# Delta-rule attention and cosine-routed experts in one kernel: units of two sequences on a written schedule, paired 64x64 products, an 8-row base of the triangular inverse

## Chip, cores and metric

The kernel runs on one core of a Trainium2 chip. The metric is device time in microseconds; the program runs once per measurement, and the figure for the kernel before is the median of three runs.

## The reference

```python
# attention: (B, H, S, D) = (4, 8, 768, 48)
k_n = k / (np.linalg.norm(k, axis=-1, keepdims=True) + 1e-06)
for t in range(S):
    y[:, :, t] = np.einsum('bhd,bhde->bhe', q[:, :, t], state)
    v_old = np.einsum('bhde,bhd->bhe', state, kt)
    state = state + bt[:, :, :, None] * np.einsum('bhd,bhe->bhde', kt, vt - v_old)
# x = y as (B*S, H*D) = (3072, 384); E, F = 8, 1024
logits = xn @ en.T / tau
expert_idx = np.argmax(logits, axis=1)
out[mask] = gate_w[mask, None] * (np.maximum(x[mask] @ w1[e], 0.0) @ w2[e])
```

`kt`, `vt`, `bt` are the normalised key, the value and beta of step t; `xn`, `en` are normalised rows, `gate_w` is the softmax probability of the chosen expert. All data are float32.

## The kernel before

The recurrence is worked in 12 chunks of 64 steps. A partition holds one step; the two halves of 64 partitions hold two of the four sequences, so a chunk is two **units** (u = 0, 1) of two sequences with eight heads each. Within a chunk the recurrence becomes a triangular system: `products` multiplies the normalised keys by themselves and the queries by the keys (a Gram matrix per head, in PSUM), DVE multiplies it with beta and a triangular mask into LM (L271). POOL masks LM further: XT, the first 4x4 blocks (L275), XTI = XT + I (L277), and for each level s = 4, 8, 16, 32 the block below the diagonal, AN (L280). The inverse grows from these: `x_plain` turns XT by a product with the identity, `x_square` and `base` give the inverse of the 4x4 blocks, and then `lower(s)` and `grow(s)` double the size of the block, up to `last`. T_ and W are the inverse and its transpose, Pm the step's factor (L325); ACT copies T_ out of PSUM, DVE copies W.

`back(c)` needs the state that chunk c-1 left: `of_state` multiplies keys and queries with the state S_all, `solve` applies the inverse, `state` updates S_all, `outputs` gives the tokens (xc), `x_transposes` and `logits` their routing scores. Every second chunk `route` picks the expert of 256 tokens, writes them to x_dram and scatters their numbers into idmap by indirect DMAs on POOL's queue. `prep` (L225) computes the keys' norms: squares and a power on POOL, sum and reciprocal on DVE, then the scaled keys KK and beta's mask MM on POOL.

A 64x64 product of one unit is 16 matmuls (eight heads, two halves); each half of the partitions uses one 64x64 tile of TensorE's array, so most products use two of the four tiles, while `grow` and `base` issue two products in turns on all four.

The order on PE is written by hand (`manual_schedule`): `front(c + 1)` runs its steps for both units, one step after the other, and after every second step one step of `back(c)` is put in. The queues of the other engines are ordered by a scheduler that follows the order of the code. All PSUM tiles come from one ring of eight banks. SP issues the loads of K, Q and V two chunks ahead.

After attention the experts' tiles of 128 tokens are counted (L526 to L556) and 31 tiles run, each with its w1 and w2 fetched by `fetch` (L559).

Of the kernel before, what the change touches and what calls it, by code (L numbers as in the profile page):

```python
# [15 lines left out]
C = 64  # L16
T = 128
LEVELS = (4, 8, 16, 32)
# [3 lines left out]
def kernel(  # L22
# [30 lines left out]

    nc = tc.nc
# [13 lines left out]
    def bank(shape):  # L68
        return ps.tile(shape, F32, name="bank", tag="bank", bufs=8)
# [68 lines left out]
    upper = ac.tile([128, 1, C], F32, name="upper")  # L138
    nc.vector.tensor_tensor(upper[:, 0, :], col_f, trow_f, op=ALU.is_gt)
    nupper = ac.tile([128, C], F32, name="nupper")  # L140
    nc.vector.tensor_scalar_mul(nupper, upper[:, 0, :], -1.0)
    nmask = {}
    for s in (0,) + LEVELS:
        m = ac.tile([128, 1, C], F32, name=f"nmask{s}")
        nc.vector.scalar_tensor_tensor(out=m[:, 0, :], in0=xor_f, scalar=float(s), in1=nupper,
                                       op0=ALU.is_ge, op1=ALU.mult)
        nc.vector.scalar_tensor_tensor(out=m[:, 0, :], in0=xor_f, scalar=float(2 * s if s else LEVELS[0]),
                                       in1=m[:, 0, :], op0=ALU.is_lt, op1=ALU.mult)
        nmask[s] = m
    id64h = id64.broadcast_to([128, H, C])  # L150


    Qp, KK, MM = [], [], []
    for i in range(2):
        t = ac.tile([128, NU, H, C], F32, name=f"Qp{i}")
        nc.gpsimd.memset(t, 0.0)
        Qp.append(t)
    for i in range(4):
        t = ac.tile([128, 2, H, C], F32, name=f"KK{i}")
        nc.vector.memset(t, 0.0)  # L160
        KK.append(t)
    for i in range(4):

        MM.append(ac.tile([128, H, C], F32, name=f"MM{i}"))
    S_all = ac.tile([128, NU, NP, 2, D], F32, name="S_all")
    nc.vector.memset(S_all, 0.0)

    def load(c):
        K4 = io.tile([128, NU, H, D], F32, name="K4", tag="K4")
        V4 = io.tile([128, NU, H, D], F32, name="V4", tag="V4", bufs=3)  # L170
        for b in range(B):
            p, u = slice(b % 2 * C, b % 2 * C + C), b // 2
            for dst, src in ((K4[p, u], k), (Qp[c % 2][p, u, :, 0:D], q), (V4[p, u], v)):
                nc.sync.dma_start(out=dst, in_=src[b, :, c * C:(c + 1) * C, :].rearrange("h p d -> p h d"))
        return K4, V4
# [7 lines left out]
    loaded = {0: load(0)}  # L183
# [35 lines left out]

    HALF = (slice(0, C), slice(C, 2 * C))  # L220

    def mm(out, lhsT, rhs, start=True):
        nc.tensor.matmul(out, lhsT=lhsT, rhs=rhs, start=start, stop=True, skip_group_check=True)  # L223

    def prep(c, K4):  # L225

        Ksq = wk.tile([128, NU, H, D], F32, name="Ksq", tag="Ksq", bufs=1)
        nc.gpsimd.tensor_tensor(Ksq, K4, K4, op=ALU.mult)
        rn = wk.tile([128, NU, H], F32, name="rn", tag="rn")
        nc.vector.tensor_reduce(rn, Ksq, axis=AX.X, op=ALU.add)  # L230
        nc.gpsimd.tensor_tensor(out=rn, in0=rn, in1=half, op=ALU.pow)
        nc.vector.tensor_scalar_add(rn, rn, 1e-6)
        nc.vector.reciprocal(rn, rn)
        for u in range(NU):
            kk = KK[(c * NU + u) % len(KK)]
            nc.gpsimd.tensor_tensor(kk[:, 0, :, 0:D], K4[:, u],  # L236
                                    rn[:, u].unsqueeze(2).broadcast_to([128, H, D]), op=ALU.mult)
            nc.gpsimd.tensor_tensor(MM[(c * NU + u) % len(MM)], upper.broadcast_to([128, H, C]),
                                    betaT[:, c, u].unsqueeze(2).broadcast_to([128, H, C]), op=ALU.mult)
            nc.gpsimd.tensor_tensor(kk[:, 1, :, 0:D], kk[:, 0, :, 0:D],  # L240
                                    betaT[:, c, u].unsqueeze(2).broadcast_to([128, H, D]), op=ALU.mult)

    def front(c):

        us = range(NU)
        KT, LM, XT, XTI, X, X2, T_, W, AN, Pm = ({} for _ in range(10))

        def transposes():
            for u in us:
                kk = KK[(c * NU + u) % len(KK)]  # L250
                KT[u] = wk.tile([128, NP, 2, 128], F32, name="KT", tag="KT", bufs=4)
                for i, src in enumerate((kk[:, 0], Qp[c % 2][:, u])):
                    psT = bank([128, NP, 128])
                    for j in range(NP):
                        nc.tensor.transpose(psT[:, j, :], src[:, 2 * j:2 * j + 2, :].rearrange("p h d -> p (h d)"),  # L255
                                            ident)
                    nc.scalar.activation(KT[u][:, :, i, :], psT, ACT.Copy)

        def products():
            for u in us:  # L260

                LM[u] = wk.tile([128, 2, NP, 2, C], F32, name="LM", tag="LM", bufs=4)
                psG = [bank([128, NP, 2, C]) for _ in range(2)]
                for j in range(NP):
                    for jj in range(2):
                        pr = slice(jj * C, jj * C + D)
                        for i in range(2):
                            mm(psG[jj][HALF[i], j], KT[u][pr, j, 0, HALF[i]], KT[u][pr, j, :, HALF[i]])
                mv = MM[(c * NU + u) % len(MM)].rearrange("p (j jj) t -> p jj j t", jj=2)
                for jj in range(2):  # L270
                    nc.vector.tensor_tensor(LM[u][:, jj], psG[jj],  # L271
                                            mv[:, jj].unsqueeze(2).broadcast_to([128, NP, 2, C]), op=ALU.mult)
                A = LM[u][:, :, :, 0, :].rearrange("p jj j t -> p (jj j) t")
                XT[u] = wk.tile([128, H, C], F32, name="XT", tag="XT", bufs=2)
                nc.gpsimd.tensor_tensor(XT[u], A, nmask[0].broadcast_to([128, H, C]), op=ALU.mult)  # L275
                XTI[u] = wk.tile([128, H, C], F32, name="XTI", tag="XTI", bufs=2)
                nc.gpsimd.tensor_tensor(XTI[u], XT[u], id64h, op=ALU.add)  # L277
                for s in LEVELS:
                    AN[u, s] = wk.tile([128, H, C], F32, name=f"AN{s}", tag=f"AN{s}")
                    nc.gpsimd.tensor_tensor(AN[u, s], A, nmask[s].broadcast_to([128, H, C]), op=ALU.mult)  # L280

        def x_plain():
            for u in us:
                p = bank([128, H, C])
                for h in range(H):
                    for i in range(2):
                        mm(p[HALF[i], h], XT[u][HALF[i], h], id64[HALF[i], 0])
                X[u] = wk.tile([128, H, C], F32, name="X", tag="X", bufs=2)
                nc.scalar.activation(X[u], p, ACT.Copy)

        def x_square():
            for u in us:
                p = bank([128, H, C])
                for h in range(H):
                    for i in range(2):
                        mm(p[HALF[i], h], XT[u][HALF[i], h], X[u][HALF[i], h])
                X2[u] = wk.tile([128, H, C], F32, name="X2", tag="X2", bufs=2)
                nc.vector.tensor_tensor(X2[u], p, id64h, op=ALU.add)  # L298

        def new_t(u, p):  # L300
            T_[u] = wk.tile([128, H, C], F32, name="T_", tag="T_", bufs=3)
            nc.scalar.activation(T_[u], p, ACT.Copy)

        def new_w(u, p):
            W[u] = wk.tile([128, H, C], F32, name="W", tag="W", bufs=6)
            nc.vector.tensor_copy(W[u], p)  # L306

        def base():
            for u in us:
                pt, pw = bank([128, H, C]), bank([128, H, C])  # L310
                for h in range(H):
                    for i in range(2):
                        mm(pt[HALF[i], h], XTI[u][HALF[i], h], X2[u][HALF[i], h])
                        mm(pw[HALF[1 - i], h], X2[u][HALF[i], h], XTI[u][HALF[i], h])
                new_t(u, pt)
                new_w(u, pw)

        def lower(s):
            for u in us:
                p = bank([128, H, C])  # L320
                for h in range(H):
                    for i in range(2):
                        mm(p[HALF[1 - i], h], AN[u, s][HALF[i], h], T_[u][HALF[i], h])
# [25 lines left out]
        for s in LEVELS[:-1]:  # L349
            steps += [lambda s=s: lower(s), lambda s=s: grow(s)]  # L350
# [288 lines left out]
```

## Time and profile before

| | us |
|---|---|
| median of three runs (1068.6 to 1071.74) | 1071.63 |
| profiled execution | 1073.31 |
| its span, first to last instruction | 1071.5 |
| of it, start, to the first transposes | 20.35 |
| attention, to the last logits | 659.27 |
| last routing and tile counts | 28.28 |
| experts | 363.60 |

Times in the profile are microseconds from the span's start. PE is TensorE's matmul rows, PEld its weight loads; DVE is VectorE, ACT ScalarE, POOL GpSimd, SP SyncE. An f32 matmul leaves two MATMUL and two LDWEIGHTS records. The profile was taken in one execution. A time in brackets behind a row of the timeline is how long the engine stood before it, and for whom; "issue" means that it waited for nothing that the profile shows.

### The profile page before, as it was taken

How to read it: one execution, taken by the hardware profiler on the slowest of the kernel's cores; microseconds unless marked ns; L12 is line 12 of the kernel's file. 1: busy time of each engine (PE TensorE's matmuls, PEld its weight loads, DVE VectorE, ACT ScalarE, POOL GpSimd, SP SyncE). 2: the span in 40 equal slices, each digit the busy share in tenths (PEclk: the TensorE clock that was granted, in tenths of full speed). 3: DMA queues.
4: the chain of work that ended last, by engine and by line, in shares of the span. 5: the costliest groups of instructions: out<-in, count | busy, mean ns of one | idle time of the engine just before them, and what ended most of it. 6: DMA issues, size and time to landing. Idle time of an engine off the chain costs nothing. (4 is left out here: it accounts for less than half of the span.)

```text
span 1071.5 us, 39767 instructions
## 1 busy us (share of the span) xinstructions
PE 820.4 (77%) x18454; PEld 729.8 (68%) x18454; DVE 312.7 (29%) x664; ACT 197.0 (18%) x381; POOL 388.9 (36%) x350
## 2 busy tenths in 40 slices
PE   2575968486948685878487868309999999999996
PEld 2475858486847685777477757308878787878784
DVE  5242436143614262535242524301010101001010
ACT  1121313131312231223122222100101010111110
POOL 6958171728171817271705070111111121212110
PEclk9787979698969896989698979759999999999999
DMA  6121012202120203011200000169999999999970
GB/s 117 32 44 32 18 33 48 32 4 47 36 43 5 47 24 55 4 33 26 39 5 3 12 24 4 31 239 336 326 322 335 323 325 325 327 320 323 325 230 1
DMA packets 135448, 130.11 MB, mean 121 GB/s; under 512 B 85738, under 2 KB 120721, under 8 KB 135282
## 3 DMA queue, kind: packets, MB, share of 16 engines
q1 hardware_dynamic: 128738, 116.55, 36.4%
q0 software_dynamic: 4736, 10.85, 3.1%
q8 instruction: 145, 2.38, 1.0%
q10 hardware_dynamic: 1808, 0.16, 0.1%
q14 instruction: 21, 0.17, 0.1%
HBM read 117.91 MB, written 10.95 MB: 120 GB/s over the span
## 5 line engine op out<-in xcount | busy, mean ns | idle before, releaser
L588 PE MATMUL bank<-xTm,w 128*128 128x128 f32 x1488 | 173.5, 277 | 0.0
L588 PEld LDWEIGHTS bank<-xTm,w 128*128 128x128 f32 x1488 | 171.1, 194 | 0.3
L593 PE MATMUL bank<-w,hT 128*128 128x384 f32 x496 | 165.1, 486 | 0.0
L223 PE MATMUL bank<-W,Pm 64*64 64x64 f32 x3072 | 115.6, 231 | 27.8 <-DVE Pm L325 21.2
L593 PEld LDWEIGHTS bank<-w,hT 128*128 128x128 f32 x496 | 91.9, 190 | 57.5
L223 PEld LDWEIGHTS bank<-W,Pm 64*64 64x64 f32 x3072 | 105.6, 145 | 33.6 <-DVE Pm L325 23.9
L223 PE MATMUL bank<-id,XT 64*64 64x64 f32 x768 | 42.0, 287 | 103.8 <-POOL XT L275 102.5
L280 POOL TENSOR_TENSOR AN<-LM,nmask 128x512 f32<-128x512 f32 x96 | 120.0, 1269 | 0.3
L223 PEld LDWEIGHTS bank<-id,XT 64*64 64x64 f32 x768 | 37.6, 195 | 107.5 <-POOL XT L275 105.6
L595 DVE TENSOR_SCALAR y<-bank,xg 128x384 f32<-128x384 f32 x31 | 19.1, 618 | 305.4 <-PE bank L593 305.4
L590 ACT ACTIVATE hT<-bank 128x512 f32<-128x512 f32 x62 | 37.0, 597 | 339.0 <-PE bank L588 339.0
L223 PE MATMUL bank<-Pm,W 64*64 64x64 f32 x2304 | 89.9, 233 | 7.9 <-issue 7.5
L596 POOL DMA_INDIRECT out_dram<-y,ids x31 | 31.5, 1015 | 167.2 <-DVE y L595 165.3
L223 PEld LDWEIGHTS bank<-Pm,W 64*64 64x64 f32 x2304 | 81.9, 145 | 8.4 <-issue 8.4
L306 DVE COPY W<-bank 128x512 f32<-128x512 f32 x96 | 65.0, 685 | 65.9 <-PE bank L223 65.9
L325 DVE TENSOR_TENSOR Pm<-bank,id 128x512 f32<-128x512 f32 x96 | 65.5, 689 | 48.8 <-PE bank L223 48.8
L569 POOL DMA_INDIRECT xg<-x_dram,ids x31 | 30.1, 970 | 134.7 <-DMA ids<-idmap 78.4
L236 POOL TENSOR_TENSOR KK<-K,rn 128x384 f32<-128x384 f32 x24 | 19.8, 831 | 141.2 <-PE bank L255 138.8
L298 DVE TENSOR_TENSOR X<-bank,id 128x512 f32<-128x512 f32 x24 | 16.6, 692 | 168.1 <-PE bank L223 168.1
L490 POOL DMA_INDIRECT idmap<-tokid,slot_i x24 | 24.2, 1006 | 66.5 <-DMA idmap<-tokid,slot_i 33.8
L578 PE MATMUL bank<-ident,xg 128*128 128x128 f32 x93 | 16.0, 283 | 39.4 <-DMA xg<-x_dram,ids 39.4
L578 PEld LDWEIGHTS bank<-ident,xg 128*128 128x128 f32 x93 | 12.3, 146 | 49.0 <-issue 36.3
(436 smaller groups left out, 1252.5 us busy)
## 6 DMA issues: line engine op xcount, KB each, us to landing
w<-in_moe_w_dram SPq DMA_DIRECT2D x62, 1536.0 KB
x_dram<-xc SPq DMA_DIRECT2D x24, 192.5 KB
K<-in_k_dram SPq DMA_DIRECT2D x48, 96.0 KB
V<-in_v_dram SPq DMA_DIRECT2D x48, 96.0 KB
Qp<-in_q_dram SPq DMA_DIRECT2D x48, 96.0 KB
ids<-idmap SPq DMA_DIRECT2D x31, 0.5 KB
xg<-x_dram,ids POOLq DMA_INDIRECT x31, 6.9
out_dram<-y,ids POOLq DMA_INDIRECT x31, 7.4
```

What stands on the lines that cost most here:

```text
L223: nc.tensor.matmul(out, lhsT=lhsT, rhs=rhs, start=start, stop=True, skip_group_check=True)
L236: nc.gpsimd.tensor_tensor(kk[:, 0, :, 0:D], K4[:, u], rn[:, u].unsqueeze(2).broadcast_to([128, H, D]), op=ALU.mult)
L280: nc.gpsimd.tensor_tensor(AN[u, s], A, nmask[s].broadcast_to([128, H, C]), op=ALU.mult)
L306: nc.vector.tensor_copy(W[u], p)
L325: nc.vector.tensor_tensor(Pm[u], p, id64h, op=ALU.add)
L490: nc.gpsimd.indirect_dma_start(out=idmap[:, :], out_offset=bass.IndirectOffsetOnAxis(ap=slot_i[:, g:g + 1], axis=0), in_=tokid[:, c - 1 + ...
L569: nc.gpsimd.indirect_dma_start(out=x, out_offset=None, in_=x_dram[:, :], in_offset=bass.IndirectOffsetOnAxis(ap=ids[:, 0:1], axis=0))
L578: nc.tensor.transpose(psX[:, j, :], x[:, j * 128:(j + 1) * 128], ident)
L588: nc.tensor.matmul(psH[:, i, :], lhsT=w1[:, j, (f + i) * 128:(f + i + 1) * 128], rhs=xT[:, j, :], start=(j == 0), stop=(j == KC - 1))
L590: nc.scalar.activation(hT[:, f:f + 4, :], psH, ACT.Relu)
L593: nc.tensor.matmul(psO, lhsT=hT[:, f, :], rhs=w2[:, f, :], start=(f == 0), stop=(f == NF - 1))
L596: nc.gpsimd.indirect_dma_start(out=out[:, :], out_offset=bass.IndirectOffsetOnAxis(ap=ids[:, 0:1], axis=0), in_=y, in_offset=None, bounds_ ...
```

## The change

Only attention changes. Its 24 units (12 chunks of two) run as a pipeline: unit n enters eight slots after unit n-1, and a list PLAN says at which slot of a unit each of its steps stands. All steps of all units are sorted by slot; steps at the same slot are issued on PE in turns, two matmuls of one and two of the other. At slot 0 modulo 8 these are first_w of one unit and solve of another, at 2 square and level 32, at 4 level 16 and outputs, at 5 fourth and last, at 6 square_t and level 8. The two products of such a pair use different tiles of the array (`from_other`, `to_other`).

Keys and values are scaled with the square root of beta, so that the Gram matrix is symmetric and its lower and upper part are read from one product. The products of keys with keys and of queries with keys are now separate 64-column matmuls. ACT copies both out of PSUM, negated (G); DVE writes the 8x8 diagonal blocks into YT and YI with copy_predicated, four instructions of 256 columns a unit, into tiles filled once with -I and I. The base is a block of eight rows, from powers: square_t, square, fourth, first_w. The level of 4 is gone. `level(s)` writes its result with copy_predicated through a mask into a tile filled with I, so that AN and its masks are not made; POOL keeps one mask per unit, M. The beta-scaled keys and MM are gone; a power of beta and a scaling of V come to POOL.

The outputs' two parts, from the state and from within the chunk, are added up in PSUM (yb, two banks of their own); the ring of the others has six banks. `k_state`, `q_state`, `solve`, `state`, `outputs`, `x_transposes` and `logits` do per unit what `of_state` to `logits` did per chunk, with the same matmuls, except that `logits` halves its columns. K and Q are loaded 42 slots ahead of the unit's slot 0, V 12. At the start POOL zeroes twelve tiles of 512 columns and DVE fills eleven.

The core of the diff; lines taken out are shown only where a number changes, and "..." stands where lines are left out:

```diff
-LEVELS = (4, 8, 16, 32)
+LEVELS = (8, 16, 32)
+BLOCK = 8
...
-        return ps.tile(shape, F32, name="bank", tag="bank", bufs=8)
+        return ps.tile(shape, F32, name="bank", tag="bank", bufs=6)
+
+    def yb():
+        t = ps.tile([128, 512], F32, name="yb", tag="yb", bufs=2)
+        return t[:, 0:NP * D].rearrange("p (j d) -> p j d", j=NP)
...
+    up8 = mask("up8", nupper[:, 0, :], 0, BLOCK)
+    lo8 = mask("lo8", lower, 0, BLOCK)
+    below = {s: mask(f"below{s}", lower, s, 2 * s) for s in LEVELS}
+    KK = filled("KK", 8, None)
+    Qp = [filled(f"Qp{i}_", NU, None) for i in range(2)]
+    YT = filled("YT", 3, -1.0)
+    YI = filled("YI", 2, 1.0)
+    PP = {s: filled(f"P{s}_", 2, 1.0) for s in LEVELS}
...
+    def prep(U):
...
+        nc.vector.tensor_tensor(rn, rn, sqb[c][:, u], op=ALU.mult)
+        U["K"] = KK[U["n"] % len(KK)]
+        nc.gpsimd.tensor_tensor(U["K"][:, :, 0:D], K, rn.unsqueeze(2).broadcast_to([128, H, D]), op=ALU.mult)
+    def scale_v(U):
+        V = V4s[U["c"]][:, U["u"]]
+        nc.gpsimd.tensor_tensor(V, V, sqb[U["c"]][:, U["u"]].unsqueeze(2).broadcast_to([128, H, D]), op=ALU.mult)
+        U["R"] = V
...
+    def gram(U):
+        KT, ps = U["KT"], [bank([128, 2, NP, C]) for _ in range(2)]
+        groups = []
+        for j in range(NP):
+            for a in range(2):
+                g = []
                 for jj in range(2):
+                    pr = slice(jj * C, jj * C + D)
                     for i in range(2):
+                        g.append((ps[jj][HALF[i if a else 1 - i], a, j], KT[pr, j, 0, HALF[i]],
+                                  KT[pr, j, a, HALF[i]], True))
+                groups.append(g)
+        def after():
+            n = U["n"]
+            U["G"] = wk.tile([128, 2, 2, NP, C], F32, name="G", tag="G", bufs=6)
+            U["YT"], U["YI"] = YT[n % len(YT)], YI[n % len(YI)]
+            for jj in range(2):
+                js = slice(jj * NP, jj * NP + NP)
+                nc.scalar.activation(U["G"][:, :, jj], ps[jj], ACT.Copy, scale=-1.0)
+                for t, m in ((U["YT"], up8), (U["YI"], lo8)):
+                    nc.vector.copy_predicated(t[:, js], m.broadcast_to([128, NP, C]), ps[jj][:, 0])
+            U["A"] = U["G"][:, 0].rearrange("p jj j t -> p (jj j) t")
+            U["M"] = U["G"][:, 1].rearrange("p jj j t -> p (jj j) t")
+            nc.gpsimd.tensor_tensor(U["M"], U["M"], nupper.broadcast_to(hc), op=ALU.mult)
+        return groups, after
+    def product(p, lhsT, rhs, from_other, to_other):
+        groups = []
+        for h in hs():
+            g = []
             for i in range(2):
+                f, o = HALF[1 - i if from_other else i], HALF[1 - i if to_other else i]
+                g.append((p[o, h], lhsT[f, h], rhs[f, h], True))
+            groups.append(g)
+        return groups
...
+    def square(U):
+        p = bank(hc)
+        def after():
+            U["Y2"] = work("Y2")
+            nc.vector.tensor_tensor(U["Y2"], p, id2.broadcast_to(hc), op=ALU.add)
+        return product(p, U["YT"], U["YI"], True, True), after
...
+    def first_w(U):
+        p = bank(hc)
+        def after():
+            U["W"] = work("W", 5)
+            nc.scalar.activation(U["W"], p, ACT.Copy, scale=-1.0)
+        return product(p, U["Y2"], U["YT"], True, False), after
+    def grow(U, eng_w="act"):
+        pt, pw = bank(hc), bank(hc)
+        P, W = U["P"], U["W"]
+        gt, gw = product(pt, W, P, False, True), product(pw, P, W, False, False)
+        def after():
+            U["T"] = work("T", 3)
+            evac("act", U["T"], pt)
+            U["W"] = work("W", 5)
+            evac(eng_w, U["W"], pw)
+        return [g for gs in zip(gt, gw) for g in gs], after
+    def level(U, s):
+        p = bank(hc)
+        def after():
+            U["P"] = PP[s][U["n"] % 2]
+            nc.vector.copy_predicated(U["P"], below[s].broadcast_to(hc), p)
+        return product(p, U["A"], U["T"], True, False), after
...
+    PERIOD = 8
+    PLAN = [
+        (-24, prep), (8, scale_v), (-19.5, transposes), (-15.5, gram),
+        (-10, square_t), (-6, square), (-3, fourth), (0, first_w), (3, grow),
+        (6, lambda U: level(U, 8)), (9, grow), (12, lambda U: level(U, 16)), (15, lambda U: grow(U, "dve")),
+        (18, lambda U: level(U, 32)), (21, last), (21.5, k_state), (23.5, q_state), (24, solve),
+        (26.5, state), (28, outputs), (31.5, x_transposes), (33.5, logits),
+    ]
+    events = []
+    for U in UNITS:
+        t0 = U["n"] * PERIOD
+        for at, f in PLAN:
+            events.append((t0 + at, len(events), lambda U=U, f=f: f(U)))
+        c = U["c"]
+        if U["u"] == 0:
+            if c > 0:
+                events.append((t0 - 42, len(events), lambda c=c: K4s.update({c: load_kq(c)})))
+            events.append((t0 - 12, len(events), lambda c=c: V4s.update({c: load_v(c)})))
+        elif c % 2 == 1:
+            events.append((t0 + 34, len(events), lambda c=c: route(c, *outs[c // 2])))
+    events.sort(key=lambda e: e[:2])
...
+        while events:
+            now = [events.pop(0)]
+            while events and events[0][0] == now[0][0]:
+                now.append(events.pop(0))
+            done = [r for r in (e[2]() for e in now) if r is not None]
+            groups = [g for g, _ in done]
+            while any(groups):
+                for g in groups:
+                    if g:
+                        for out_, lhsT, rhs, start in g.pop(0):
+                            nc.tensor.matmul(out_, lhsT=lhsT, rhs=rhs, start=start, stop=True,
+                                             skip_group_check=True)
+            for _, after in done:
+                after()
```

## Rows read from the trace of the kernel before

**Rows 1.** Windows by stage: us, busy (records) of PE, PEld, DVE, ACT, POOL, clock, DMA, GB/s.

```profile
0.00:20.35 20.35, 1.30 (x9) 1.10 (x9) 14.63 (x49) 1.90 (x3) 13.20 (x25) 1.00 0.66 117
20.35:679.62 659.27, 478.31 (x16364) 455.87 (x16364) 256.27 (x508) 157.83 (x315) 310.24 (x260) 0.86 0.15 28
679.62:707.90 28.28, 1.03 (x4) 0.93 (x4) 8.08 (x46) 0.23 (x1) 4.92 (x5) 0.52 0.19 49
707.90:1071.50 363.60, 339.74 (x2077) 271.89 (x2077) 33.72 (x62) 37.02 (x62) 60.54 (x61) 0.96 0.88 297
```

**Rows 2.** What PE waited for in 30 to 680: us, times, longest.

```profile
PE bank L223 <- POOL XT L275: 100.6, 18, 7.3
PE bank L223 <- issue: 55.1, 66, 2.2
```

**Rows 3.** Windows, the stretch around two waits for XT.

```profile
405.50:419.00 13.50, 2.24 (x36) 1.93 (x36) 0.27 (x1) 1.35 (x3) 10.69 (x10) 0.57 0.47 66
```

**Rows 4.** Timeline of PE: start, us, first instruction after a wait, [wait].

```profile
434.46 0.21 PE L223 MATMUL bank<-W,Pm 64*64 64x64 f32 x1 [1.55 <-issue]
...
438.43 0.27 PE L223 MATMUL bank<-T__6896,AN 64*64 64x64 f32 x2 [0.83 <-issue]
...
441.90 0.27 PE L223 MATMUL bank<-W,Pm 64*64 64x64 f32 x1 [0.44 <-issue]
```

**Rows 5.** Windows cut where PE stood for "issue".

```profile
430.72:434.46 3.74, 2.19 (x128) 2.06 (x128) 1.39 (x3) 0.00 (x0) 3.55 (x2) 1.00 0.02 4
434.46:438.43 3.97, 3.14 (x129) 3.00 (x128) 3.14 (x7) 1.20 (x2) 0.97 (x2) 1.00 0.02 4
438.43:441.90 3.47, 3.03 (x128) 2.89 (x129) 1.81 (x3) 1.23 (x4) 0.00 (x0) 1.00 0.02 5
441.90:445.87 3.97, 3.08 (x128) 2.97 (x128) 2.07 (x3) 1.20 (x2) 0.00 (x0) 1.00 0.02 4
445.87:449.61 3.74, 3.03 (x128) 2.66 (x128) 1.39 (x2) 1.47 (x3) 0.00 (x0) 1.00 0.02 4
```

**Rows 6.** The page, parts 1 and 3: PE's records; queue 8's packets and MB.

```profile
PE 820.4 (77%) x18454; PEld 729.8 (68%) x18454; DVE 312.7 (29%) x664; ACT 197.0 (18%) x381; POOL 388.9 (36%) x350
...
q8 instruction: 145, 2.38, 1.0%
```

**Rows 7.** DMA in 430 to 450: all packets of all queues.

```profile
DMA packets 5, 0.08 MB, mean 4 GB/s; under 512 B 0, under 2 KB 0, under 8 KB 0
```

**Rows 8.** Groups by line, 20 to 680: shapes, count, busy us, mean ns, idle before.

```profile
L223 PE MATMUL bank<-S_all,KT 48*64 48x48 f32 x1408 | 26.0, 218 | 5.1 <-issue 5.0
...
L223 PE MATMUL bank<-KT 48*64 48x128 f32 x768 | 25.2, 279 | 0.0
...
L255 PE MATMUL bank<-ident,KK 128*128 128x128 f32 x96 | 17.3, 309 | 5.6 <-POOL KK L236 5.6
```

**Rows 9.** Windows, within a grow.

```profile
333.62:334.55 0.93, 0.93 (x69) 0.93 (x72) 0.39 (x2) 0.61 (x4) 0.00 (x0) 1.00 0.00 0
```

**Rows 10.** Timeline of PE: a two-tile product at the low and the high clock.

```profile
410.41 1.97 PE L223 MATMUL bank<-id,XT 64*64 64x64 f32 x32 [4.68 <-POOL XT L275]
...
660.14 1.15 PE L223 MATMUL bank<-T__10724,AN 64*64 64x64 f32 x32
```

**Rows 11.** Groups by line, 0 to 690, DVE, ACT and POOL.

```profile
L280 POOL TENSOR_TENSOR AN<-LM,nmask 128x512 f32<-128x512 f32 x96 | 120.0, 1269 | 0.3
...
L325 DVE TENSOR_TENSOR Pm<-bank,id 128x512 f32<-128x512 f32 x96 | 65.5, 689 | 48.8 <-PE bank L223 48.8
L306 DVE COPY W<-bank 128x512 f32<-128x512 f32 x96 | 65.0, 685 | 65.9 <-PE bank L223 65.9
...
L231 POOL TENSOR_TENSOR rn<-rn,half 128x16 f32<-128x16 f32 x12 | 35.0, 2916 | 20.5 <-DVE rn L230 20.5
...
L257 ACT ACTIVATE KT<-bank 128x512 f32<-128x512 f32 x48 | 25.4, 601 | 23.0 <-PE bank L255 22.9
...
L236 POOL TENSOR_TENSOR KK<-K,rn 128x384 f32<-128x384 f32 x24 | 19.8, 831 | 141.2 <-PE bank L255 138.8 <-DVE rn L233 2.1
```

More of the change, by code (lines that the diff above doesn't have):

```diff
@@ L150 @@
[L150 to L159, printed above, removed]
-        nc.vector.memset(t, 0.0)
[L161 to L166, printed above, removed]
@@ L220 @@
     HALF = (slice(0, C), slice(C, 2 * C))
[L222 to L229, printed above, removed]
+    UNITS = [dict(n=n, c=n // NU, u=n % NU) for n in range(NC * NU)]
+    sqb = {}
+    outs = {}
@@ new lines, in hs, with work @@
+    def hs():
+        return range(H)
+    def work(name, bufs=2, cols=C):
+        return wk.tile([128, H, cols], F32, name=name, tag=name, bufs=bufs)
+    def prep(U):
+        c, u = U["c"], U["u"]
+        if u == 0:
+            sqb[c] = wk.tile([128, NU, H], F32, name="sqb", tag="sqb", bufs=4)
+            nc.gpsimd.tensor_tensor(out=sqb[c], in0=betaT[:, c], in1=half, op=ALU.pow)
+        K = K4s[c][:, u]
+        Ksq = wk.tile([128, H, D], F32, name="Ksq", tag="Ksq", bufs=1)
+        nc.gpsimd.tensor_tensor(Ksq, K, K, op=ALU.mult)
+        rn = wk.tile([128, H], F32, name="rn", tag="rn")
@@ L230, in prep @@
         nc.vector.tensor_reduce(rn, Ksq, axis=AX.X, op=ALU.add)
-        nc.gpsimd.tensor_tensor(out=rn, in0=rn, in1=half, op=ALU.pow)
+        nc.gpsimd.tensor_tensor(out=rn, in0=rn, in1=half[:, 0], op=ALU.pow)
         nc.vector.tensor_scalar_add(rn, rn, 1e-6)
         nc.vector.reciprocal(rn, rn)
[L234 to L241, printed above, removed]
@@ new lines, in k_state, with after @@
+    def k_state(U):
+        if U["c"] == 0:
+            return [], lambda: None
+        p, groups = of_state(U, 0)
+        def after():
+            V = U["R"].rearrange("p (j jj) d -> p jj j d", jj=2)
+            U["R"] = wk.tile([128, H, D], F32, name="R", tag="R")
+            for jj in range(2):
+                nc.vector.tensor_tensor(U["R"].rearrange("p (j jj) d -> p jj j d", jj=2)[:, jj], V[:, jj], p[jj],
+                                        op=ALU.subtract)
+        return groups, after
@@ new lines, in q_state, with solve, after @@
+    def q_state(U):
+        if U["c"] == 0:
+            U["psY"] = [yb(), yb()]
+            return [], lambda: None
+        U["psY"], groups = of_state(U, 1)
+        return groups, lambda: None
+    def solve(U):
+        p = bank([128, H, D])
+        groups = [[(p[HALF[i], h], U["W"][HALF[i], h % 2 * NP + h // 2], U["R"][HALF[i], h], True)
+                   for i in range(2)] for h in hs()]
+        def after():
+            U["Z"] = wk.tile([128, H, D], F32, name="Z", tag="Z")
+            evac("act", U["Z"], p)
+        return groups, after
@@ new lines, in outputs, with after @@
+    def outputs(U):
+        c, u = U["c"], U["u"]
+        if u == 0 and c % 2 == 0:
+            outs[c // 2] = (io.tile([128, 2, NU, Dm + 1], F32, name="xc", tag="xc"),
+                            wk.tile([128, 2, NU], F32, name="ssx", tag="ssx"),
+                            wk.tile([128, 2, NU, E], F32, name="lz", tag="lz"))
+        xc, ssx, _ = outs[c // 2]
+        p = U["psY"]
+        groups = [[(p[h % 2][HALF[i], h // 2], U["M"][HALF[i], h % 2 * NP + h // 2], U["Z"][HALF[i], h],
+                    c == 0 and h < 2) for i in range(2)] for h in hs()]
+        def after():
+            U["x"] = xc[:, c % 2, u, 0:Dm]
+            for jj in range(2):
+                evac("act", U["x"].rearrange("p (j jj d) -> p jj j d", jj=2, d=D)[:, jj], p[jj])
+            ysq = wk.tile([128, Dm], F32, name="ysq", tag="ysq", bufs=1)
+            nc.scalar.activation(ysq, U["x"], ACT.Square, accum_out=ssx[:, c % 2, u:u + 1])
+        return groups, after
@@ new lines, in x_transposes, with logits, after @@
+    def x_transposes(U):
+        psX = bank([128, KC, 128])
+        for j in range(KC):
+            nc.tensor.transpose(psX[:, j, :], U["x"][:, j * 128:(j + 1) * 128], ident)
+        U["xT"] = wk.tile([128, KC, 128], F32, name="xT", tag="xT")
+        nc.scalar.activation(U["xT"], psX, ACT.Copy)
+    def logits(U):
+        p = bank([128, E])
+        groups = [[(p[HALF[i]], U["xT"][:, j, HALF[i]], enT[:, j, :], j == 0) for i in range(2)] for j in range(KC)]
+        def after():
+            nc.vector.tensor_copy(outs[U["c"] // 2][2][:, U["c"] % 2, U["u"]], p)
+        return groups, after
```

307 lines of the change are left out of this document (98 added, 209 removed).

## The prediction

> **What bounds the kernel now.** Read the stages first [rows 1]: 20.35 us of start, 659.27 us of attention, 28.28 us in which the last tokens are routed and the experts' tiles counted, 363.60 us of experts. The change touches attention and its start alone; the last two stages (391.9 us) stay as they are, since the experts' first tile cannot be looked up before the last token is routed, and their stage is at a DMA share of 0.88. So everything turns on the 659 us. There PE is busy 478 us with 16,364 MATMUL records, every other engine under half.
>
> Why is PE, the busiest, not busy always? The waits of PE [rows 2] name two things. One is POOL: 18 times PE sits, 5.6 us on average, until POOL has masked the Gram products into XT. The stretch around such a wait shows what follows from it: 13.5 us with 36 records and a granted clock of 0.57 [rows 3], a mix of its two levels, 1.2 and 2.4 GHz. The other is called "issue", 66 times and 55.1 us: PE waited for nothing that the profile shows.
>
> The second I take to be the supply of PE's instructions, and the whole forecast hangs on it, so here are its rows. In a dense stretch at clock 1.00 the waits named "issue" come at 434.46, 438.43 and 441.90 [rows 4]. Cut the time at these points and at the two after: each piece holds 128 MATMUL and 128 LDWEIGHTS (within one) and lasts 3.47 to 3.97 us, **whatever is in it** [rows 5]. The first piece has 2.19 us of PE work, the third 3.03, and the piece with less work isn't shorter. Two times 18,454 PE instructions against 145 instruction packets of 2.38 MB on queue 8 [rows 6] are 255 to a packet, at 64 bytes each; and in 20 us of this stretch five packets moved, and nothing else [rows 7], for five crossings. So PE runs blocks of 256 instructions, the next is fetched while one runs, and a fetch takes about 18.89 / 5 = 3.8 us from crossing to crossing; a block with less work than that ends in a stall. Per record: 18.89 us / 641 = **29.5 ns**.
>
> **The change, part by part.** Unit = two sequences, one chunk; there are 24.
>
> *PE instructions.* A 64x64 f32 product of one unit is 16 matmuls and leaves 32 records: KT x768 is 24 units times 16 times 2 [rows 8]. A transpose leaves one (96 for 24 times 4 [rows 8]). Counted from the diff, per unit: transposes 8 + 3; gram 64 (it was 32: 64 columns instead of 128 to a matmul); square_t, square, fourth, first_w 128; three grows 192; three levels 96; last 32; solve 32; outputs 32; logits 12 (was 6); k_state, q_state, state 32 each in 22 of 24 units. The sum is 24 x 599 + 22 x 96 = 16,488, and 20 of routing: 16,508. Before it was 16,364. x_plain, the level of 4 and the old base go, but what comes is as long: **the change makes no instruction go away**. It makes them denser.
>
> *PE work.* Four tiles at once: 69 records in 0.93 us in a grow [rows 9]. Two at once: 32 records in 1.15 us, of which the last record's own 0.22 is a tail [rows 10], so 0.93 as well. Paired as the plan pairs them (first_w with solve, square with level 32, level 16 with outputs, fourth with last, square_t with level 8), five pairs and three grows take 8 x 0.93 = 7.4 us. Gram: half of a 128-column record's 25.2 / 768 us, times 64, is 1.05. State products 96 x 26.0 / 1408 = 1.8 [rows 8]. Transposes and logits, 23 records at no more than 17.3 / 96 = 0.18, 4.1. Together 14.4 us a unit at the most.
>
> *PE's blocks.* 687 records a unit at 29.5 ns are 20.3 us. That is more than 14.4, so the pairing saves work where it was not the limit. For all of them: 16,508 x 29.5 ns = **487 us**.
>
> *The wait on POOL goes.* Four AN, XT and XTI at 1.27 us [rows 11] and MM leave POOL; masking is done by copy_predicated from PSUM on DVE. What POOL keeps per unit is Ksq, K and V scaled (0.83 each), a power of 8 columns (half to all of 2.92), half the power for beta (1.46) and one mask (1.27), with about 1 us of scatter: 7.9 to 9.3 us. Its chain for a unit's K may start when the Gram of two units before is read, 11 slots ahead of its use; the chain is about 6 us, a slot (an eighth of a unit) 2.5 us. So nothing waits. What is next late is the instruction block.
>
> *copy_predicated* is in no row. It reads a mask in SBUF and data in PSUM, as Pm does (0.69 us for 512): low end. High end: the slowest 512-element row of two inputs, POOL's AN, 1.27. A gain below the low end is excluded: W's copy, with one input fewer, takes 0.69 too [rows 11]. I take 0.69, since engine and sources are the same. DVE per unit: copy_predicated 4 x 256 + 3 x 512, two sums and a W of 512, R, S and the norm's sum of 384 each: 5,248 elements at 1.35 ns = 7.1, and some eleven small ones (norms, logits, a quarter of a routing) at 0.2: 9.3 us; at the high end 12.2. ACT: KT and G 1024 each, eight copies of 512, Z, x, its square and xT of 384 each: 7,680 elements at 601 / 512 ns [rows 11], 9.0 us. All under 20.3: **free**, and they would matter only if the blocks came faster. The smaller banks ring (six, for 24 banks a unit) lets PE run three steps ahead of the readers, 7 us, against two or three readings of 0.6 to 0.7 each; free too.
>
> *Loads.* The same DMAs, issued 18 to 22 slots ahead (over 40 us), V apart from K and Q; SP's queue also holds the writes of x_dram, which wait for routing, but the plan puts the next loads ten slots behind them. No cost.
>
> *Start.* POOL's zeroing grows from 2 x 1024 columns to 12 x 512, DVE fills eleven tiles of 512 for four memsets; halved norm steps give some back. I put 2 us on it: 22.4.
>
> *Fill and drain.* The plan runs 24 units plus 43 slots of tail and head. At the head POOL does the units' norms one after the other (6 us each, with M), three between the first transposes and the fourth unit's: 24 us with some, against 470 records = 13.9 us. I put 12 us on it. At the end the last unit's nine dependent steps at about 2 us (0.93 product, 0.60 copy, the hand-overs) are 18 to 22 us, against some 620 records = 18: 4 us.
>
> *Sum.* 22.4 + 487 + 16 + 391.9 = 917 us of span; the profiled execution lasted 1073.31 for a span of 1071.5, so 1.8 lies around it: 919. The median of the runs, 1071.63, is 1.7 under the profiled one. **Forecast: 920 us**, attention going from 659 to about 503.
>
> **Rivals.**
> 1. *Blocks arrive in time.* Then a unit costs what PE works, 14.4 us: 24 x 14.4 = 346, with 35 of fill and drain 381, and 22.4 + 381 + 391.9 + 1.8 = 797 us; if 14.4 is too high as well, DVE's 12.2 gives 744. For it: 16,364 records are 128 blocks, and PE's waits name "issue" only 66 times, so half of the crossings stalled nothing. Against it: the block of 2.19 us of work that lasted 3.74. 0.07. The Trainium skill has this as its rule ("Runtime: NRT & Kernel Launch", section "Instruction fetch mechanics"): an engine fetches the next 256 instructions while it runs the present ones, and crossing a block is "mostly hidden". This trace agrees with the 256, and with the hiding only where a block holds more than 3.8 us of work.
> 2. *Blocks set the pace, but the clock halves.* In the piece with the least work the clock stayed at 1.00 [rows 5], after a wait of 4.7 us for XT it was 0.57 over the stretch [rows 3]; all attention would now look like the former, and whether the clock stays up over a whole stage of such pieces no row shows. At the low level a 32-record product took 1.97 us against 1.15 [rows 10]; 14.4 x 1.71 = 24.6 us a unit is over 20.3, so PE's work is the limit: 24 x 24.6 + 16 = 606, and 1022 us. In part, 960 to 1022. 0.13.
> 3. *Slower: PE, in its fixed order, waits for K or masks as it did for XT.* The place is transposes(U) behind POOL's norm chain, which passes to DVE and back twice, in queues that other units now share. At the low clock (24.6 us) it decides from 26.8 - 24.6 = 2.2 us of wait a unit, where 26.8 = (659.27 - 16) / 24 is what a unit may cost for the old time. At the old wait, 5.6 us, a unit is 30.2 and the whole 22.4 + 741 + 393.7 = 1157 us. Against it: 11 slots of lead for a chain of 6 us. 0.05.
> 4. *The pairs don't run side by side.* Then five pairs cost 1.86 instead of 0.93, a unit 14.4 + 4.7 = 19.1 us: still under 20.3, and the time is the same. It has no chance of its own.
>
> **How the numbers follow.** The forecast, with blocks between 3.7 and 4.1 us (a fetch beside loads is longer; the pieces go from 3.47 to 3.97) and fill and drain from 5 to 30 us, covers 890 to 960: 0.70. Rivals 1, 2 and 3: 0.07, 0.13, 0.05. Fetches partly overlapped, 800 to 890: 0.04; at the old time by chance 0.01. A range of 885 to 1000 leaves out rival 1 and the overlap (0.11), rival 3 (0.05) and the upper end of rival 2. Differences of less than 0.3% this kernel's times can't tell from none. Faster by more 0.94, same 0.01, slower 0.05.
>
> **What would show it.** Right: in the profile after, attention of about 500 us with some 16,500 records, PE's largest wait "issue", at every 128th record, pieces of 3.8 us with 2 to 2.5 us of work, no wait on POOL over 1 us between unit 4 and unit 22. Wrong: pieces of 128 records well under 3.4 us (rival 1); a granted clock near 0.5 in the middle of attention (rival 2); waits on K or G by PE (rival 3); a copy_predicated over 1.3 us.

## The result and the profile after

The changed kernel takes 978.32 us (median of four, 977.07 to 980.52) where the kernel before takes 1071.68 on the same chip: a ratio of **0.9137**, 95% interval 0.9114 to 0.916. Forecast were 920 us with a range of 885 to 1000. On a second chip the same two kernels gave 0.9112 (0.9069 to 0.9156). Chips differ (before took 1057 to 1072 us on the four that were used), so the experiments are compared by their ratio to before, and the changed kernel counts as 0.911 to 0.914.

The profiled execution has a span of 975.3 us. First the windows by stage, as in [rows 1]: us, then busy us and records of PE, PEld, DVE, ACT and POOL, granted clock, DMA share, GB/s.

```profile
0.00:35.54 35.54, 1.30 (x9) 1.11 (x9) 17.63 (x65) 1.90 (x3) 26.55 (x39) 1.00 0.35 63
35.54:583.60 548.06, 393.79 (x16508) 359.16 (x16508) 210.76 (x569) 206.98 (x437) 170.87 (x148) 0.89 0.18 34
583.60:611.90 28.30, 1.03 (x4) 0.93 (x4) 8.32 (x47) 0.23 (x1) 4.79 (x6) 0.52 0.19 49
611.90:975.30 363.40, 339.96 (x2077) 272.13 (x2077) 33.72 (x62) 37.04 (x62) 60.62 (x62) 0.96 0.87 298
```

Attention fell by 111.2 us, to 548.06 where some 503 were forecast; the start grew by 15.2 us, where 2 were forecast; the last two stages are what they were. The whole miss, 58 us, is 45 us of attention and 13 us of start. What PE waited for (us, times, longest), against [rows 2]:

```profile
PE bank L588 <- issue: 106.0, 99, 3.2
...
PE yb L588 <- issue: 16.9, 18, 2.5
...
PE bank L292 <- POOL KK L280: 14.8, 1, 14.8
PE bank L535 <- DVE den L524: 13.6, 6, 2.7
PE bank L292 <- issue: 4.5, 3, 2.2
...
PE bank L482 <- issue: 1.7, 1, 1.7
```

The waits for POOL in the middle of attention are gone; the one for KK is the first unit's, in the start. The four rows of "issue" come to 129.1 us in 121 waits, where the kernel before had 55.1 in 66; attention has 129 blocks, so now nearly every crossing stands. Work that got denser ended in the same blocks. The next fence has windows cut where PE stood for "issue", as in [rows 5], from a dense stretch of the changed kernel:

```profile
319.54:323.28 3.74, 2.14 (x128) 2.00 (x128) 1.35 (x3) 0.60 (x1) 0.00 (x0) 1.00 0.18 32
323.28:327.03 3.75, 2.73 (x128) 2.36 (x129) 0.69 (x1) 1.96 (x4) 0.00 (x0) 1.00 0.02 4
327.03:330.50 3.47, 2.40 (x128) 2.24 (x128) 1.44 (x4) 2.06 (x4) 1.15 (x1) 1.00 0.02 5
330.50:334.17 3.67, 2.35 (x127) 2.19 (x127) 2.31 (x6) 0.00 (x0) 0.94 (x2) 1.00 0.02 4
```

128 records take 3.5 to 3.75 us at full clock, as before, now with 2.1 to 2.7 us of PE work in them where [rows 5] had 2.2 to 3.1. Next, for PE alone (us, busy, records, clock, DMA share, GB/s), two blocks at the clock's low level, 0.50: there the work nearly fills the block, and the block is longer.

```profile
303.10:307.60 4.50, 3.84 (x128) 0.50 0.01 0
307.90:312.30 4.40, 4.26 (x131) 0.50 0.00 0
```

Two places that the forecast had not costed. The POOL timeline of the start (start, us, instruction): four powers of beta, of which the first unit needs one, stand before its scaled K.

```profile
22.41 0.83 POOL L272 TENSOR_TENSOR Ksq<-K 128x384 f32<-128x384 f32 x1
23.20 11.50 POOL L269 TENSOR_TENSOR sqb<-betaT,half 128x16 f32<-128x16 f32 x4
34.66 1.62 POOL L280 TENSOR_TENSOR KK<-K,rn 128x384 f32<-128x384 f32 x2
```

And PE's timeline around one routing: the logits are issued at 187.65; the next in PE's fixed order is the rank product of the routing. It reads `oh`, the chosen expert, which DVE has at 190.02, at the end of a chain of small steps behind the logits; the profile names den, the sum of ACT's exponentials, which ends beside it.

```profile
187.65 0.52 PE L588 MATMUL bank<-enT,xT 128*64 128x8 f32 x12
...
189.84 0.18 DVE L517 TENSOR_TENSOR oh<-first,pref_e 128x32 f32<-128x32 f32 x1
...
190.16 0.61 PE L535 MATMUL bank<-oh,mask_su 128*128 128x32 f32 x2 [1.99 <-DVE den L524]
```

The new operations, by group (count, busy us, mean ns, idle before):

```profile
L389 DVE COPY_PREDICATED P<-below,bank 128x512 f32<-128x512 int32 x72 | 53.0, 736 | 71.3 <-PE bank L588 62.3 <-PE yb L588 8.7
...
L317 DVE COPY_PREDICATED YT<-up,bank 128x256 f32<-128x256 int32 x48 | 21.2, 442 | 98.8 <-ACT G L315 98.8
```

### The profile page after: what moved, and what is told of

The parts are those of the page before. It is cut to its first block, busy times and chain, and to the rows that moved or that the text cites. A ratio compares the mean times of both kernels' runs of the same rounds, so it can differ in the third digit from the quotient of the medians.

```text
span 975.3 us, 40125 instructions
## 1 busy us (share of the span) xinstructions
PE 736.1 (75%) x18598; PEld 633.3 (65%) x18598; DVE 270.4 (28%) x742; ACT 246.2 (25%) x503; POOL 262.8 (27%) x252
## 5 line engine op out<-in xcount | busy, mean ns | idle before, releaser
L588 PE MATMUL bank<-T,G 64*64 64x64 f32 x2304 | 103.3, 240 | 18.8 <-issue 17.7
L588 PE MATMUL bank<-W,P 64*64 64x64 f32 x2304 | 98.0, 231 | 23.2 <-issue 22.6
L588 PEld LDWEIGHTS bank<-T,G 64*64 64x64 f32 x2304 | 89.8, 152 | 22.8 <-issue 21.0
L588 PEld LDWEIGHTS bank<-W,P 64*64 64x64 f32 x2304 | 84.9, 144 | 28.8 <-issue 27.0
L336 ACT ACTIVATE T<-bank 128x512 f32<-128x512 f32 x72 | 43.1, 598 | 167.6 <-PE bank L588 162.7
L588 PE MATMUL bank<-P,W 64*64 64x64 f32 x1536 | 67.0, 234 | 17.0 <-issue 15.8
L389 DVE COPY_PREDICATED P<-below,bank 128x512 f32<-128x512 int32 x72 | 53.0, 736 | 71.3 <-PE bank L588 62.3
L588 PEld LDWEIGHTS bank<-P,W 64*64 64x64 f32 x1536 | 58.6, 147 | 20.1 <-issue 18.8
L588 PE MATMUL bank<-KT 48*64 48x64 f32 x1536 | 38.2, 243 | 11.3 <-issue 10.9
L275 POOL TENSOR_TENSOR rn<-rn,half 128x8 f32<-128x8 f32 x24 | 39.5, 1646 | 24.8 <-DVE rn L274 24.1
```

The lines of the kernel that those rows point to most:

```text
L275: nc.gpsimd.tensor_tensor(out=rn, in0=rn, in1=half[:, 0], op=ALU.pow)
L336: nc.scalar.activation(out, p, ACT.Copy)
L389: nc.vector.copy_predicated(U["P"], below[s].broadcast_to(hc), p)
L588: nc.tensor.matmul(out_, lhsT=lhsT, rhs=rhs, start=start, stop=True, skip_group_check=True)
```

## Experiments

**Theory.** In attention PE is paced by blocks of 256 instructions. The gain came from the waits for XT that went, not from pairing; the shortfall is the start's powers, the routing's place in PE's order, and blocks at the low clock. **Rival.** PE's columns or the evacuations set the pace, and the pairing made the gain. The stages shown below for the runs end at the last rank product, some 3 us behind the last logits; taken that way the changed kernel's own is 551.4 us on the chip of the result and 542.3 on the second one.

**More columns, same records.** In `product`:

```
-                g.append((p[o, h], lhsT[f, h], rhs[f, h], True))
+                wide = slice(h * C, h * C + (96 if h < H - 1 else C))
+                g.append((p.rearrange("p h t -> p (h t)")[o, wide], lhsT[f, h],
+                          rhs.rearrange("p h t -> p (h t)")[f, wide], True))
```

> The changed kernel, but each of the 14 products of a unit that are written out head by head streams 96 columns instead of 64 for seven heads of eight (the next head overwrites the surplus). PE has the same 16,508 records, with some 44% more columns in two thirds of them: about 3 us more work a unit, 72 us in all. If the supply of PE's instructions sets the pace of attention: attention stays within 2% of 548 us, the whole within 1% of 978 us. If PE's work sets it: attention about 615 to 620 us, the whole 1045 to 1055 us.

Measured: 975.85 us, 0.9205 of before (0.9165 to 0.9244), so 0.7 to 1.0% over the changed kernel, just clear of the intervals, where the rival wanted 7%. Its attention stage:

```profile
35.51:589.90 554.39, 434.34 (x16511) 402.77 (x16512) 213.02 (x583) 208.57 (x438) 170.97 (x148) 0.94 0.17 33
```

40 us more of PE work (72 were expected, so the rival's price comes down to some 4%) and a granted clock of 0.94 instead of 0.89, in almost the same time. Columns are not the pace at full clock.

**Half the records, same columns.** Only even heads are issued, each over two heads' columns, which gives the odd heads the wrong weights:

```
-                g.append((p[o, h], lhsT[f, h], rhs[f, h], True))
+                if h % 2 == 0:
+                    g.append((p[o, h:h + 2], lhsT[f, h], rhs[f, h:h + 2], True))
```

> The changed kernel, but each of those products is written with half the instructions: only even heads are issued, each over the 128 columns of two heads, so the odd heads are multiplied with the wrong weights. Columns, evacuations and waits stay; records fall from 16,508 to about 11,130, a unit from 687 to 463. If the supply of instructions sets the pace: a unit falls from 22.2 us to between 14.5 us (PE's own work) and 16 us, attention from 548 to 400 to 430 us, the whole to 830 to 860 us. If PE's columns or the evacuations set it: attention stays near 548 us.

Measured: 857.97 us, 0.8108 (0.8074 to 0.8142), within the expectation as it stands; at this ratio the chip of the result would give 869, a little over it. The stage, and the waits:

```profile
35.50:470.70 435.20, 349.10 (x11135) 315.87 (x11136) 212.14 (x583) 204.19 (x438) 170.31 (x148) 0.93 0.21 41
```

```profile
PE bank L590 <- DVE P L391: 33.2, 16, 4.8
...
PE bank L590 <- issue: 11.0, 16, 1.4
```

5,376 records fewer took some 107 us away, and this row of "issue" fell from 106.0 to 11.0, all of them from 129.1 to 22.0. So records are what attention costs, but at 20 ns each and not at 29.5: once blocks hold more work, the work and the hand-over to DVE's P (33.2 us, 3.7 in the changed kernel) come up behind them.

**The pairs apart.** The steps of one slot are issued one after the other:

```
-            while any(groups):
-                for g in groups:
+            for g in groups:
+                while g:
```

> The changed kernel, but steps that stand in the same slot are issued one after the other instead of alternately, so five pairs of products a unit no longer use all four tiles at once (the three grows still do). If the supply of instructions sets the pace: 14.4 + 4.7 = 19.1 us of work a unit is still under the 20.3 us of the blocks, and the whole moves by less than 1.5% (0 to +15 us). If the pairing is what made the change faster: 24 x 4.7 = 112 us more, the whole near 1090 us, as slow as before.

Measured: 972.11 us, 0.9187 (0.9147 to 0.9227): 5 to 8 us over the changed kernel, hardly more than the interval. The stage:

```profile
35.50:580.00 544.50, 443.87 (x16512) 415.86 (x16512) 216.29 (x583) 210.52 (x438) 170.65 (x148) 0.94 0.18 34
```

Five pairs a unit without their four tiles cost nearly nothing, though PE has 50 us more of work; again a clock of 0.94.

**The kernel before without its waits.** First XT alone (DVE masks it, and the masks of the levels come after both XTI):

```
-                nc.gpsimd.tensor_tensor(XT[u], A, nmask[0].broadcast_to([128, H, C]), op=ALU.mult)
+                nc.vector.tensor_tensor(XT[u], A, nmask[0].broadcast_to([128, H, C]), op=ALU.mult)
...
-                for s in LEVELS:
+            for s in LEVELS:
+                for u in us:
```

> The kernel before, with two edits: XT is masked by DVE instead of POOL, and POOL builds the masks of the levels only after XTI of both units. If the waits of PE for POOL's XT (100.6 us in 18) and the low clock after them are what the change took away: the old kernel falls by 70 to 95 us to 975 to 1000 us, level with the changed one. If the gain is the denser pairing: it falls by less than 30 us.

Measured: 1003.24 us, 0.9474 (0.9442 to 0.9505): 56 us less, short of the 70 to 95. What PE waited for, against [rows 2]:

```profile
PE bank L223 <- DVE Pm L327: 52.6, 11, 7.6
...
PE bank L223 <- POOL XTI L277: 17.4, 13, 3.8
PE bank L223 <- DVE XT L275: 11.9, 9, 3.4
```

A wait that goes uncovers the next. Pm is late because DVE, in order, stands in the norm's chain for POOL's power. The timeline of one such place:

```profile
244.91 2.91 POOL L231 TENSOR_TENSOR rn<-rn,half 128x16 f32<-128x16 f32 x1 [1.07 <-DVE rn L230]
...
247.85 0.79 DVE L232 TENSOR_SCALAR rn<-rn 128x16 f32<-128x16 f32 x1 [2.42 <-POOL rn L231]
...
249.40 1.27 DVE L327 TENSOR_TENSOR Pm<-bank,id 128x512 f32<-128x512 f32 x2
```

So a second version, with XTI on DVE as well, and the norm as one power:

```
-        nc.gpsimd.tensor_tensor(out=rn, in0=rn, in1=half, op=ALU.pow)
-        nc.vector.tensor_scalar_add(rn, rn, 1e-6)
-        nc.vector.reciprocal(rn, rn)
+        nc.gpsimd.tensor_tensor(out=rn, in0=rn, in1=nhalf, op=ALU.pow)
```

> The kernel before, with XT and XTI both on DVE, the masks of the levels after them, and the norm as one power of -0.5 on POOL, so that DVE no longer stands in the norm's chain with Pm behind it (11 waits of 52.6 us in the run without the XT wait). 16,364 records, and no pair that the change brought. If the change gains by the waits alone: 955 to 980 us, level with the changed kernel. If its pairing is worth something of its own: it stays above 990 us.

Measured: 984.11 us, 0.930 (0.9253 to 0.9346), just above the band that was named for "waits alone" and under the 990 of the rival. On this chip the change is worth 91 us, and 73 of them come here from the waits, with the old records and no new pair. Its attention is 32 us longer than the changed kernel's on the same chip (574.20 against 542.30), its start 16.5 shorter (19.00 against 35.5). What is left in attention is in its waits:

```profile
PE bank L225 <- DVE X L300: 17.1, 4, 6.2
PE bank L225 <- DVE XT L275: 16.2, 12, 2.2
PE bank L225 <- DVE Pm L327: 14.0, 5, 4.7
```

47 us, which the pipeline over units in the changed kernel doesn't have. That they make up the 32 us is argued from this fence, not tried.

**The routing later.** `route` ends after the writes of x_dram; the rank products and what follows are a function of their own:

```
             events.append((t0 + 34, len(events), lambda c=c: route(c, *outs[c // 2])))
+            events.append((t0 + 39.25, len(events), lambda c=c: place(c)))
```

> The changed kernel, with the routing of two chunks cut in two: its softmax part stays in its slot, PE's two rank products and all that follows them are issued 5.25 slots (about 14 us) later in PE's fixed order. Where the changed kernel stood 11.3 us in five waits for that softmax and some 10 us more in the slow clock after them: if the route's place in PE's order is a part of the shortfall, no wait of PE for the softmax remains and the whole falls by 10 to 25 us against the changed kernel's 0.914 of before, to 0.89 to 0.905. If the blocks of instructions swallow it: less than 4 us.

Measured: 964.78 us, 0.9089 (0.9044 to 0.9134), 2 to 5 us less: within the interval, and a miss. The waits:

```profile
PE bank L600 <- issue: 112.5, 102, 3.7
...
PE yb L600 <- issue: 12.4, 11, 1.8
PE bank L600 <- DVE P L389: 9.1, 4, 3.6
...
PE bank L546 <- DVE den L524: 2.3, 1, 2.3
PE bank L292 <- issue: 1.5, 1, 1.5
```

The wait went as meant (13.6 to 2.3, the last one having nothing to stand behind). It did not go into block crossings: all rows of "issue" come to 126.4 us against 129.1. The wait for DVE's P grew from 3.7 to 9.1, and where the rest went isn't shown. That the routing's place is a part of the shortfall is not borne out beyond these 2 to 5 us.

**Square roots at the start.**

```
-            nc.gpsimd.tensor_tensor(out=sqb[c], in0=betaT[:, c], in1=half, op=ALU.pow)
+            sqb[c] = sqall[:, c]
...
+    nc.scalar.activation(sqall, betaT, ACT.Sqrt)
```

> The changed kernel, with the square roots of beta taken once for all chunks by ACT at the start instead of by POOL, chunk by chunk. If the four powers that POOL ran ahead of the first unit's scaled K (11.5 us) are what made the start 35.5 us long: the first transposes come 10 to 12 us earlier, the start is about 24 us, and the whole falls by 10 to 13 us (0.901 to 0.905 of before). If the first loads or PE's wait for the experts' embeddings are as late: under 4 us.

Measured: 953.69 us, 0.8982 (0.8921 to 0.9043), 14 to 16 us less, a little over what was expected. The start is 25.10 us:

```profile
0.00:25.10 25.10, 1.32 (x10) 1.13 (x10) 17.59 (x65) 3.54 (x5) 15.17 (x35) 1.00 0.49 90
```

10.4 us of the gain are the start, as expected; a few more are in attention, within what attention differs between chips (551.4 and 542.3 us for the changed kernel itself).

**Gram with half the instructions.**

```
-                        g.append((ps[jj][HALF[i if a else 1 - i], a, j], KT[pr, j, 0, HALF[i]], KT[pr, j, a, HALF[i]], True))
+                    g.append((ps[jj][HALF[i], :, j], KT[pr, j, 0, HALF[i]], KT[pr, j, :, HALF[i]], True))
```

> The changed kernel with the Gram products written as in the kernel before, 128 columns to a matmul, which takes 32 of a unit's 687 records away (768 in all) and leaves the columns as they were; the halves that the later products go through are exchanged to suit, by which one pair a unit (fourth with last) loses its four tiles, 0.93 us of work. If the supply of instructions sets the pace: 768 x 29.5 ns = 22.7 us less, at the measured block price 768/128 x 4.18 = 25 us less, so 0.890 to 0.895 of before. If PE's work sets it: 24 x 0.93 = 22 us more, 0.935.

Measured: 954.36 us, 0.8984 (0.8928 to 0.904): 14 to 16 us less, short of the 23 to 25 expected, against 22 more by the rival. Per record 18 to 21 ns, as in the run with half the records.

**No loads.**

```
-                events.append((t0 - 42, len(events), lambda c=c: K4s.update({c: load_kq(c)})))
+                events.append((t0 - 42, len(events), lambda c=c: K4s.update({c: load_kq(c) if c < 2 else K4s[c % 2]})))
```

> The changed kernel without the loads of K, Q and V from the third chunk on: chunks 2 to 7 work on what chunks 0 and 1 brought. Instructions of the engines as before but for the DMA issues of SP. If fetches beside loads are what lifts the mean block from its median of 3.8 us to 4.18: attention falls by 15 to 40 us. If the long blocks come from waits and from the slow clock: less than 8 us.

V is treated likewise. Measured: 966.12 us, 0.9104 (0.9059 to 0.9149): 1 to 4 us less. The stage and two waits that the changed kernel doesn't have at this length:

```profile
35.50:583.30 547.80, 379.53 (x16512) 347.04 (x16512) 219.31 (x583) 207.20 (x438) 170.94 (x148) 0.93 0.05 11
```

```profile
PE bank L588 <- DVE rn L277: 11.9, 1, 11.9
...
PE bank L588 <- DVE YI L317: 8.3, 1, 8.3
```

The DMA share fell from 0.18 to 0.05 and the time stayed. But the profiled execution took 973.13 us, 7 over the median, with 20 us of new waits in it, so a small effect of loads on the fetch is not excluded.

**The changed kernel again, and two versions that put the findings together.**

> The changed kernel as it is, on the chip of the next three, so that they can be set against it and not only against the kernel before: 0.914 of before again, 965 to 972 us where before takes 1060.

Measured: 966.1 us, 0.9112 (0.9069 to 0.9156), as expected.

> The later routing, the square roots at the start, the 128-column Gram products together, and the logits as three matmuls of all 128 tokens instead of six of 64 (6 records a unit less). By the single runs: 6 + 17 + 16 us, and 144 records x 29.5 ns = 4 us: 43 us under the changed kernel, near 925 us, 0.873 of before. If they hide one another (the earlier start ends in the same waits, the shorter blocks stall where the route stood): no better than 940 us.

Measured: 925.67 us, 0.8743 (0.8715 to 0.8772): 40 us under the changed kernel on the same chip, where 43 were expected. The edits add up, as far as the interval (3 us each way) can tell.

> As the last one, and the two products with the state, for K and for Q, as one matmul of 128 stationary columns each (32 records a unit less in 22 units, 704 in all); V and the last W go through the other half to suit, ACT copies K and Q once more into the order needed, and R and x are read in four pieces instead of two. If records are what attention costs: 704 x 29.5 ns = 20.8 us less than the last, near 905 us, 0.853 of before. If ACT or DVE, with some 1.5 us a unit more, or PE's work (now near the blocks) is the limit: within 6 us of it.

Its core (KX holds K and Q of one sequence side by side), the rest being halves exchanged to suit:

```
+                    w = U["KX"][pr, j, 2 * i:2 * i + 2].rearrange("p a t -> p (a t)")
+                    g.append((p[jj][i][:, j], w, S_u[U["u"]][pr, j, i], j == 0 and i == 0))
```

Measured: **914.21 us**, 0.8643 (0.8609 to 0.8677), 52 us under the changed kernel and the fastest here. 704 records fewer gave 11.5 us, 16 ns each: between its two expectations. Its start and attention:

```profile
0.00:25.30 25.30, 1.30 (x9) 1.10 (x9) 17.75 (x66) 3.54 (x5) 15.20 (x35) 1.00 0.51 87
25.30:527.00 501.70, 413.17 (x14895) 382.20 (x14896) 230.13 (x627) 246.17 (x532) 147.65 (x140) 0.93 0.19 36
```

## Why the prediction was right, and where it was off

*The forecast.* The range of 885 to 1000 held because it took in a part of rival 2; the 890 to 960 that the forecast's own terms were to cover was missed by 18 us.

*Blocks of instructions set the pace: right.* Columns added, pairs taken apart: nothing over 1%; records taken away: 18 to 21, 20 and 16 ns for each, in three runs. That is roughly two thirds of 29.5, and why it isn't more was not tried. The Trainium skill's "mostly hidden" ("Runtime: NRT & Kernel Launch", section "Instruction fetch mechanics") does not hold here: 121 waits named "issue" at 129 blocks, 129.1 us, say that a crossing stalls nearly every time.

*The count: right*, 16,508 records of 16,508. *The price: too low, and this is the term that failed.* Between the fill and the drain, 121 of attention's 129 blocks, from fetch to fetch of queue 8, take 4.15 us on average and not 3.78: 121 x 0.37 = 45 us, the whole miss in attention. The other 8 blocks have 46 us, 30 at 3.78 and 16 of fill and drain, the two terms put on those. Sorted by what is in them:

- 80 at full clock: 3.94 us, 12.5 us in excess. Their median is 3.76, the forecast's price; four blocks of over 5 us make two thirds of the excess.
- 36 at the low clock for a part: 4.34 us, 20.1 us in excess. In the two blocks shown at 0.50 PE works 3.84 and 4.26 us, more than 3.78: rival 2's mechanism, which then met a part of a third of the blocks. The time lies in its band, and 0.13 was too little for it. The 29.5 ns came from a stretch at clock 1.00 alone. But two blocks of 8 us make 8.4 of the 20.1, and one of them holds a wait of 3.0 us for DVE's YI.
- 5 with a routing: 6.27 us, 12.5 us in excess. Rival 3 had the mechanism, a wait in PE's fixed order, but looked for it at K and the masks. The wait took 11.3 us in those five, and in the run with the routing moved it went and gave back no more than 5.

The sorting shows where the excess lies, not what would be saved without it: the routing's 12.5 us gave back 2 to 5, and the two runs with half the time at the low clock, which had 40 and 50 us more of PE work, were not faster. So the size of the failed term is measured, and its split into causes stays open.

*POOL's wait goes: right.* The two versions of before show it: 56 and 73 us. They also show what "nothing waits" hid: one wait taken away alone lets the next (Pm, 52.6 us) come up. *copy_predicated at the low end: right*, 736 ns for 512 columns against 690, and 442 for 256. DVE, ACT and POOL have 8.8, 8.6 and 7.1 us a unit (busy time of the stage by 24) against 9.3, 9.0 and 7.9 to 9.3, and were free but for 13 us that PE stood for DVE's and ACT's results outside the routing. (POOL's terms in the working add up to 7.7 to 9.1, a unit takes 25 banks and not 24, and 919 less 1.7 is 917; none of it bears on the outcome.) *Loads at no cost: agrees*, within what that run can tell; that a fetch beside loads is longer, as the blocks' upper end of 4.1 us had it, no run shows. *Rival 4: right* to within 8 us.

*The start: wrong*, 15.2 us and not 2. The beta powers were counted as a mean of 1.46 us a unit of POOL's time, but not placed in its queue: four of them came ahead of the first K, and the run that takes them away gives 10.4 us back. The other 2.7 us over the 22.4 stay open.

## What to carry over

On this kernel a denser PE was worth next to nothing (5 to 8 us of 970), because PE was paced by its instructions: compare PE's work in 128 records with the time that they take before paying for concurrency, and if the time is the longer, look for fewer instructions (wider operands, shared stationary columns). Price the block over the whole stage, low clock and waits in the fixed order included, and not from its best stretch. A helper that prepares work ahead must be placed in its queue, not only summed: it runs ahead of the first result too.

## What the runs showed of the hardware that was not expected

With more work in the same time the clock was higher. The changed kernel's attention had a granted clock of 0.89, with 96 columns to a product 0.94, with the pairs apart 0.94, at the same records and within 1% of the time: the denser the work, the longer PE stands at the crossings (129 us of "issue" against 83 and 74), and the records of the clock show 119 us at 1.2 GHz in the changed kernel's attention against 61 and 65 us in these two. That the stands cause the falls was not tried by itself: in the changed kernel a stand of 0.8 us or more lies shortly before each of 21 falls, but most of its 89 such stands had no fall behind them. The time didn't follow the clock; that at full clock the blocks were the limit anyway is argued.

A block's 3.8 us are not the time that its packet takes. In the trace of the changed kernel, between 64 and 577 us, a packet of queue 8 takes 1.1 us (median). Of 103 waits named "issue" of 0.3 us or more, 92 end 1.2 to 1.65 us after the end of the last packet (median 1.4), and the next packet starts 1.2 us (median) after that. The three make 3.7 us, so the moving of the bytes is less than a third of a block's time. The end of the stand follows the packet, which ties "issue" to the fetch; what fills the other two parts no view shows.
